# First batch of attention in native fp32, token-mixing weights converted at set steps, first q tile loaded from another queue

## Chip, core and metric

The kernel runs on one NeuronCore of a Trainium2 chip. The metric is the device time of one launch in microseconds (us), the median of several runs; lower is better. Engine names are those of the profile: PE is the matrix engine (PEld its weight load), DVE the vector engine, ACT the scalar engine, POOL the GpSimd engine, SP the engine whose queue issues most transfers.

## What is computed

Three stages run one after another on four sequences of 448 positions with 768 features: causal attention with 12 heads of 64, then a mixer (over positions, then over channels), then a second mixer with a cosine and a sine.

```python
scores = scale * np.matmul(q, k.transpose(0, 1, 3, 2))        # q, k, v: (4, 12, 448, 64)
scores = np.where(mask, -1000000000.0, scores)
attn = np.exp(scores - np.max(scores, axis=-1, keepdims=True))
attn = attn / (np.sum(attn, axis=-1, keepdims=True) + 1e-09)
x = np.matmul(attn, v)                                        # to (4, 448, 768)
...
h = np.maximum(xt @ w_tok1, 0.0) @ w_tok2                     # mixer 1, over positions
u = x + h.transpose(0, 2, 1)
x = u + np.maximum(u @ w_ch1, 0.0) @ w_ch2                    # mixer 1, over channels
...
theta = x @ w_theta                                           # mixer 2
y = einsum(w_tok_r, x * cos(theta)) + einsum(w_tok_i, x * sin(theta))
u = x + y
out = u + np.maximum(u @ w_ch, 0.0)
```

The weights arrive as 64-bit floats and are turned into 32-bit ones on the chip.

## The kernel before

**Attention.** Two heads make a pair, six pairs a batch, 24 pairs in all; they are numbered 0 to 23 (`b * NPR + pr`). A pair has seven score tiles (`TILES`), so batch 0 has 42 steps `n`. `prep` loads q, k and v of a pair one pair ahead. `scores` makes one tile: the matmul of q and k into a `sc` bank (three of them), on DVE the mask and the row maximum (L268), on ACT the exponential (L270). `pv` multiplies the exponentials with v, four steps later (`LAG`), `finish` normalizes a pair and splits it into a high and a low part, and `tokmix` does the token mixing after every second pair.

There are two ways of doing each of the two products. For a pair in `NATIVE`, q and k are used as fp32 tiles whose lower 64 partitions are set to zero by POOL (`k_pad`, `q_raw`), and one fp32 matmul per tile does the scores. For any other pair q and k are loaded twice over (128 partitions) and split on ACT and DVE into a high and a low part (`qs`, `kh`, `kl`), and two fp32r matmuls do them (L261 and L263). For a pair in `NATPV`, the exponentials are transposed on PE against an identity (L277), copied out of PSUM by ACT (L279, tile `ptf`), and multiplied by v in fp32 (L305). For any other pair ACT writes them as fp16 (`ph`), DVE writes the rest (L290), a transposing transfer on SP's queue turns them (L293, `pt<-ph`), v is split in three bfloat16 parts on DVE (`v_mid`), and PE does 83 small matmuls (L316).

Before the change pair 3 is not in `NATIVE` and pair 2 is not in `NATPV`; all others of the first batch are in both. `q_raw` and `k_raw` share two buffers (tag `qk_raw`), `k_pad` and `kh` another two.

**Weights.** `load64` loads a raw tile of 64-bit floats (two `raw` buffers) and converts it: one ACT operation (L124), four on DVE (L125, L126, L128, L129). `split_w` then makes the high part on ACT (L106) and the low part on DVE (L113). `tok_weights` does so for the four tiles of the token-mixing weights, `convert_early` for the first six tiles of the channel-mixing weights from step 21 on; later ones are converted as the channel mixing needs them. A channel weight is also stored (`w_c<-ws`) and streamed again for later batches.

**Order.** The Tile framework decides the order on each engine from a timeline that it works out itself when the program is built; `high_priority(AHEAD)` puts attention ahead, and `issue_after(x)` lets what is inside come only after x in that order. On the chip each engine then takes its instructions strictly in that order, and SP issues its transfers in its order too. The channel mixing of batch 0 (`run_units`) starts in the middle of batch 1; from there on PE has other work at hand whenever attention waits.

Of the kernel before, what the change touches and what calls it, by code (L numbers as in the profile page):

```python
# [13 lines left out]
AF = mybir.ActivationFunctionType  # L14
# [4 lines left out]
P = 128  # L19
B, H, S, D = 4, 12, 448, 64  # L20
E = H * D
NPR = H // 2
# [4 lines left out]
NEG = -1.0e30  # L27
PSC = 32768.0
BUFS = dict(ut=9, h2=6, acc=12, ws=4, wf=2, raw=2, sb=3, ph=3, pt=5)
NATIVE = {0, 1, 2, 4, 5, 6, 7}  # L30
NATPV = {0, 1, 3, 4, 5, 6, 7, 8, 9, 10, 11}
AHEAD, LAG, LOOK = 500, 4, 2
KEEP, UBACK = 6, 16
LATE_CONVERT = 16
EARLY = 6
ENGINES = {
    0: dict(qhi="A", qlo="D", khi="A", klo="D", v="D", phi="A", xhi="A", xlo="D", uhi="A", ulo="D"),
}
# [10 lines left out]
def fused(ctx, tc, q, k, v, w_tok1, w_tok2, w_ch1, w_ch2, w_theta, w_tok, w_ch, out):  # L49
# [15 lines left out]
    nc = tc.nc  # L65
# [114 lines left out]
    for j in range(BUFS["sb"]):  # L180
        sb = ac.tile([P, 512], F32, tag=f"sb{j}", name=f"sb{j}")
# [4 lines left out]
    def tok_weights(n):  # L186
        if n < 2:
            cols = slice(n * 512, (n + 1) * 512)
            load_split(wt1[:, :, cols], w_tok1[:, cols])
        else:  # L190
            load_split(wt2[:, n - 2], w_tok2[:, (n - 2) * S:(n - 1) * S])
# [7 lines left out]
    loads = {}  # L199

    def prep(b, pr):
        qr = ap2.tile([P, 2 * S], F32, tag="qk_raw", name="q_raw", bufs=2)
        if b * NPR + pr in NATIVE:
            kr = ap2.tile([P, 2 * S], F32, tag="kh", name="k_pad")
            for t, src in ((kr, k), (qr, q)):
                (nc.vector if b * NPR + pr == 0 and t is kr else nc.gpsimd).memset(t[64:128], 0.0)
                loads[b * NPR + pr] = nc.sync.dma_start(out=t[0:64], in_=src[b, pr, 0:64])
        else:
            loads[b * NPR + pr] = nc.sync.dma_start(out=qr, in_=q[b, pr])
            kr = ap2.tile([P, 2 * S], F32, tag="qk_raw", name="k_raw", bufs=2)  # L210
            nc.sync.dma_start(out=kr, in_=k[b, pr])
        vr = ap2.tile([P, 9 * D], F32, tag="v_raw", name="v_raw")
        nc.sync.dma_start(out=vr, in_=v[b, pr])
        if b * NPR + pr in NATIVE:
            qs, kh, kl = qr, kr, None
        else:
            qs = ap2.tile([P, 2 * S], F32R, tag="qs", name="qs")
            copy_to(pick("qhi"), qs, qr)
            rest_to(pick("qlo"), qs[64:128], qr[64:128], qs[64:128])
            kh = ap2.tile([P, 2 * S], F32R, tag="kh", name="kh")  # L220
            copy_to(pick("khi"), kh, kr)
            kl = ap2.tile([P, 2 * S], F32R, tag="kl", name="kl")
            rest_to(pick("klo"), kl, kr, kh)
        if b * NPR + pr in NATPV:
            return qs, kh, kl, (vr,)
        v1 = vr.bitcast(BF16).rearrange("p (n w) -> p n w", w=2)[:, :, 1]
        vm = ap2.tile([P, 9 * D], F32, tag="v_mid", name="v_mid", bufs=1)
        rest_to(pick("v"), vm, vr, v1)
        v2, v3 = (vm.bitcast(BF16).rearrange("p (n w) -> p n w", w=2)[:, :, z] for z in (1, 0))
        rest_to(pick("v"), v3, vm, v2)  # L230
        return qs, kh, kl, (v1, v2, v3)
# [3 lines left out]
    class Pair:  # L235
        def __init__(self, b, pr, parts):
# [4 lines left out]
            self.pts, self.ps = {}, None  # L241
            self.native_pv = b * NPR + pr in NATPV

    def scores(pp, i, h):
        ps = bank("sc", 3)
        if i == 0:
            j, kk, nb = 6, P, 2
            n = P if pp.kl is None else 256
            lhs = pp.qs[:, 0:P]
            cut = lambda t: t.rearrange("p (h s) -> p h s", h=2)[:, :, 0:n // 2]  # L250
            src = ps[:, 0:n].rearrange("p (h s) -> p h s", h=2)[:, :, 0:64]
            msk = mask0
        else:
            j, kk, nb = (i - 1) * 2 + h, 64 + P * i, 1 + 2 * i
            n = kk if pp.kl is None else max(256, kk)
            q0 = P * (3 * h + i)
            lhs = pp.qs[:, q0:q0 + P]
            cut = lambda t: t[:, h * S:h * S + n]
            src = ps[:, 0:kk]
            msk = mask[:, S - kk:S]  # L260
        nc.tensor.matmul(ps[:, 0:n], lhsT=lhs, rhs=cut(pp.kh), start=True, stop=pp.kl is None)  # L261
        if pp.kl is not None:
            nc.tensor.matmul(ps[:, 0:n], lhsT=lhs, rhs=cut(pp.kl), start=False, stop=True)  # L263
        sb = sbufs[count[0] % BUFS["sb"]]
        count[0] += 1
        full, sb = sb, sb[:, 64:512]
        dst = sb[:, 0:P].rearrange("p (h s) -> p h s", h=2) if i == 0 else sb[:, 0:kk]
        nc.vector.tensor_tensor_reduce(out=dst, in0=src, in1=msk, op0=ALU.add, op1=ALU.min, scale=-0.125,  # L268
                                       scalar=3.0e38, accum_out=pp.mx[:, j:j + 1])
        nc.scalar.activation(sb[:, 0:kk], sb[:, 0:kk], AF.Exp, bias=pp.mx[:, j:j + 1], scale=-1.0,  # L270
                             accum_out=pp.sm[:, j:j + 1])
        if pp.native_pv:
            nt = 1 + i
            c0 = 64 if i == 0 else 0
            pst = mm_bank()
            for u in range(nt):
                nc.tensor.transpose(pst[:, u * P:(u + 1) * P], full[:, c0 + u * P:c0 + (u + 1) * P], ident)  # L277
            pt = ap2.tile([P, 4, P], F32, tag="pt", name="ptf", bufs=BUFS["pt"])
            nc.scalar.activation(pt[:, 0:nt].rearrange("p n q -> p (n q)"), pst[:, 0:nt * P], AF.Copy)  # L279
            pp.pts[i, h] = pt  # L280
            return
        ph = ap2.tile([P, 2 * S], F16, tag="ph", name="ph", bufs=BUFS["ph"])
        if i == 0:
            hi, los = ph[:, 0:P], ((ph[:, P:2 * P], 0, P),)
        else:
            hi = ph[:, 64:64 + kk]
            los = ((ph[:, 0:64], 0, 64), (ph[:, 64 + kk:2 * kk], 64, kk))
        copy_to(pick("phi"), hi, sb[:, 0:kk], PSC)
        for dst, c0, c1 in los:
            nc.vector.scalar_tensor_tensor(out=dst, in0=sb[:, c0:c1], scalar=PSC, in1=hi[:, c0:c1],  # L290
                                           op0=ALU.mult, op1=ALU.subtract)
        pt = ap2.tile([P, 7, P], F16, tag="pt", name="pt", bufs=BUFS["pt"])
        nc.sync.dma_start_transpose(out=pt[:, 0:nb, :], in_=ph[:, 0:nb * P])  # L293
        pp.pts[i, h] = pt
# [109 lines left out]
    def convert_early(n):  # L404
        while early[0] < min(n, EARLY):
            convert(*jobs[early[0]])
            early[0] += 1
# [24 lines left out]

    eng, turn = dict(ENGINES[0]), {}

# [6 lines left out]
    pairs, xgs = {}, {}  # L441
# [12 lines left out]
    for n, (b, pr, t) in enumerate(steps):  # L454
# [3 lines left out]
            pairs[b, pr] = Pair(b, pr, parts[b, pr])  # L458
        with tc.high_priority(AHEAD):
            scores(pairs[b, pr], *TILES[t])  # L460
        if b == 0 and n % 3 == 2 and n // 3 < 4:
            tok_weights(n // 3)
        if n >= 21:
            convert_early((n - 18) // 3)
        if n >= 140:
# [126 lines left out]
    for b in range(B):  # L592
        raw, x2 = [], []
        for d in range(DT):
            r = acc_tile()
            nc.sync.dma_start(out=r, in_=x2d[b][d])
            t = hl_tile("ut")
# [126 lines left out]
```

## Time and profile before

| | us |
|---|---|
| median of 3 runs | 936.4 (933.72 to 938.17) |
| the profiled execution, its own time | 932.47 |
| its span, first to last instruction | 930.7 |
| granted clock of PE over the span | 0.996 |

The profiled execution lies 3.9 us below the median of the runs and 1.25 us below the lowest of them. Outside its span lie 1.8 us. All rows below are of this one execution, in us from the start of its span. An fp32 matmul with fp32 operands leaves two records on PE, so "x8" of such a line is four matmuls; an fp32r matmul or a transpose leaves one.

### The profile page before, as it was taken

How to read it: one execution, taken by the hardware profiler on the slowest of the kernel's cores; microseconds unless marked ns; L12 is line 12 of the kernel's file. 1: busy time of each engine (PE TensorE's matmuls, PEld its weight loads, DVE VectorE, ACT ScalarE, POOL GpSimd, SP SyncE). 2: the span in 40 equal slices, each digit the busy share in tenths (PEclk: the TensorE clock that was granted, in tenths of full speed). 3: DMA queues.
4: the chain of work that ended last, by engine and by line, in shares of the span. 5: the costliest groups of instructions: out<-in, count | busy, mean ns of one | idle time of the engine just before them, and what ended most of it. 6: DMA issues, size and time to landing. Idle time of an engine off the chain costs nothing.

```text
span 930.7 us, 16002 instructions
## 1 busy us (share of the span) xinstructions
PE 901.3 (97%) x5846; PEld 822.5 (88%) x5846; DVE 637.1 (68%) x1484; ACT 389.5 (42%) x916; POOL 107.3 (12%) x176
## 2 busy tenths in 40 slices
PE   7799999999999989899999999999999999999998
PEld 5687899999988879798989899999999999999997
DVE  5998579999777776757776278855765467475351
ACT  5886676667555555435544043322211212112100
POOL 2110000000000000000000000021531243242120
PEclk9999999999999999999999999999999999999999
DMA  5888567887999988999699989863604235153043
GB/s 170 244 248 314 220 237 237 319 284 246 264 257 335 250 220 191 236 291 251 197 309 275 318 290 355 303 206 109 208 1 151 61 112 168 28 162 111 22 131 128
DMA packets 108335, 196.75 MB, mean 211 GB/s; under 512 B 65120, under 2 KB 77152, under 8 KB 108256
## 3 DMA queue, kind: packets, MB, share of 16 engines
q1 hardware_dynamic: 107104, 194.15, 68.3%
q0 software_dynamic: 1152, 1.57, 0.8%
q8 instruction: 46, 0.75, 0.3%
q14 instruction: 33, 0.27, 0.1%
HBM read 145.88 MB, written 34.60 MB: 194 GB/s over the span
## 4 chain that ended last, share of the span: by engine, by line
PE 74%; DMA 15%; DVE 7%; issue 2%; ACT 1%; SPq 1%; DVEq 0%; ACTq 0%
PE ps_mm L162 17%; PE ps_mm L160 17%; PE ps_mm L161 17%; DMA pt<-ph 11%; PE ps_pv L305 4%; PE ps_sc L261 3%; PE ps_sc L162 3%; PE ps_sc L160 3%; PE ps_sc L161 3%; PE ps_mm L277 2%; PE ps_pv L316 2%; DMA x2d<-acc 1%; DVE sb L268 1%; PE ps_sc L263 1%; DVE ph L290 1%
## 5 line engine op out<-in xcount | busy, mean ns | idle before, releaser
L162 PE MATMUL ps_mm<-h,ws 128*128 128x448 f32 x432 | 159.1, 369 | 0.0
L161 PE MATMUL ps_mm<-h,ws 128*128 128x448 f32 x432 | 158.9, 368 | 0.0
L160 PE MATMUL ps_mm<-h,ws 128*128 128x448 f32 x432 | 158.7, 368 | 0.0
L161 PE MATMUL ps_mm<-ut,ws 128*128 128x448 f32 x288 | 107.0, 372 | 0.0
L162 PE MATMUL ps_mm<-ut,ws 128*128 128x448 f32 x288 | 106.9, 372 | 0.0
L160 PE MATMUL ps_mm<-ut,ws 128*128 128x448 f32 x288 | 106.5, 371 | 0.0
L270 ACT ACTIVATE sb<-sb,mx 128x192 f32<-128x192 f32 (+3 forms) x168 | 89.1, 532 | 33.4 <-DVE mx L268 32.9
L162 PEld LDWEIGHTS ps_mm<-h,ws 128*128 128x128 f32 x432 | 81.2, 188 | 7.0
L161 PEld LDWEIGHTS ps_mm<-h,ws 128*128 128x128 f32 x432 | 81.2, 188 | 6.9
L160 PEld LDWEIGHTS ps_mm<-h,ws 128*128 128x128 f32 x432 | 81.1, 188 | 6.9 <-DVE h L378 0.2
L268 DVE CUSTOM_DVE_ANT_0 sb<-ps_sc,mask 128x192 f32<-128x192 f32 (+3 forms) x168 | 74.3, 456 | 11.5 <-PE ps_mm L277 7.2
L290 DVE SCALAR_TENSOR_TENSOR ph<-sb,ph 128x64 f16<-128x64 f32 (+3 forms) x169 | 46.2, 316 | 42.3 <-ACT ph L106 42.1
L109 POOL TENSOR_SCALAR ut<-acc 128x448 fp32r<-128x448 f32 x24 | 16.7, 704 | 472.6 <-DMA acc<-x2d 462.6
L528 ACT ACTIVATE tmp<-ps_sc 128x384 f32<-128x384 f32 x28 | 13.5, 483 | 132.3 <-PE ps_sc L162 132.1
L106 ACT ACTIVATE ph<-sb 128x192 f16<-128x192 f32 (+3 forms) x91 | 39.5, 443 | 67.8 <-DMA pt<-ph 67.3
L305 PE MATMUL ps_pv<-v_raw,ptf 128*128 128x128 f32 (+1 forms) x418 | 57.6, 276 | 2.1 <-ACT ptf L279 1.8
L160 PEld LDWEIGHTS ps_mm<-ut,ws 128*128 128x128 f32 x288 | 54.4, 189 | 5.1 <-DMA ws<-w_c 0.4
L305 PEld LDWEIGHTS ps_pv<-v_raw,ptf 128*128 128x128 f32 x418 | 53.3, 191 | 6.2 <-ACT ptf L279 3.8
L161 PEld LDWEIGHTS ps_mm<-ut,ws 128*128 128x128 f32 x288 | 54.5, 189 | 4.7 <-issue 0.2
L162 PEld LDWEIGHTS ps_mm<-ut,ws 128*128 128x128 f32 x288 | 54.4, 189 | 4.8 <-issue 0.4
L316 PEld LDWEIGHTS <-pt 128*128 128x128 f16 x1079 | 35.8, 97 | 20.5 <-DMA pt<-ph 11.9
L386 DVE TENSOR_TENSOR acc<-ps_mm,acc 128x448 f32<-128x448 f32 x48 | 29.8, 622 | 30.9 <-PE ps_mm L162 30.6
(151 smaller groups left out, 2097.6 us busy)
## 6 DMA issues: line engine op xcount, KB each, us to landing
ws<-w_c SPq DMA_DIRECT2D x102, 768.0 KB, 5.6
raw<-in_w_ch_dram SPq DMA_DIRECT2D x30, 768.0 KB, 5.7
w_c<-ws SPq DMA_DIRECT2D x30, 768.0 KB, 5.1
q_raw<-in_q_dram SPq DMA_DIRECT2D x17, 448.0 KB, 5.0
k_raw<-in_k_dram SPq DMA_DIRECT2D x17, 448.0 KB, 4.6
v_raw<-in_v_dram SPq DMA_DIRECT2D x24, 288.0 KB, 4.6
x2d<-acc SPq DMA_DIRECT2D x24, 224.0 KB, 5.2
acc<-x2d SPq DMA_DIRECT2D x24, 224.0 KB, 4.0
```

The source lines that it names most:

```text
L106: nc.scalar.activation(dst, src, AF.Copy, scale=scale)
L160: nc.tensor.matmul(ps, lhsT=ka(a[:, 0]), rhs=kb(b[:, 0]), start=first, stop=False)
L161: nc.tensor.matmul(ps, lhsT=ka(a[:, 0]), rhs=kb(b[:, 1]), start=False, stop=False)
L162: nc.tensor.matmul(ps, lhsT=ka(a[:, 1]), rhs=kb(b[:, 0]), start=False, stop=last)
L261: nc.tensor.matmul(ps[:, 0:n], lhsT=lhs, rhs=cut(pp.kh), start=True, stop=pp.kl is None)
L268: nc.vector.tensor_tensor_reduce(out=dst, in0=src, in1=msk, op0=ALU.add, op1=ALU.min, scale=-0.125, scalar=3.0e38, accum_out=pp.mx[:, j:j ...
L270: nc.scalar.activation(sb[:, 0:kk], sb[:, 0:kk], AF.Exp, bias=pp.mx[:, j:j + 1], scale=-1.0, accum_out=pp.sm[:, j:j + 1])
L277: nc.tensor.transpose(pst[:, u * P:(u + 1) * P], full[:, c0 + u * P:c0 + (u + 1) * P], ident)
L290: nc.vector.scalar_tensor_tensor(out=dst, in0=sb[:, c0:c1], scalar=PSC, in1=hi[:, c0:c1], op0=ALU.mult, op1=ALU.subtract)
L305: nc.tensor.matmul(pp.ps[:, reg:reg + n], lhsT=pt[:, u], rhs=pp.v[0][:, vt * D:vt * D + n], start=(u == 0), stop=(u == len(blks) - 1))
L316: nc.tensor.matmul(pp.ps[:, reg:reg + D], lhsT=pt[:, blk], rhs=pp.v[c][:, vt * D:(vt + 1) * D], start=(n == 0), stop=(n == len(jobs) - 1))
L386: nc.vector.tensor_tensor(out=acc[d], in0=ps[:, 0:S], in1=acc[d], op=ALU.add)
```

## The change

Pair 3 enters `NATIVE` and pair 2 enters `NATPV`, so all six pairs of batch 0 do both products in fp32. `tok_weights` is called at steps 3, 5, 8 and 10 instead of 2, 5, 8 and 11, and each call may only come behind that step's exponential. The first q tile is loaded in two pieces from ACT's queue instead of in one from SP's.

```diff
-NATIVE = {0, 1, 2, 4, 5, 6, 7}
-NATPV = {0, 1, 3, 4, 5, 6, 7, 8, 9, 10, 11}
+NATIVE = {0, 1, 2, 3, 4, 5, 6, 7}
+NATPV = {0, 1, 2, 3, 4, 5, 6, 7, 8, 9, 10, 11}
...
+TOK_STEPS = (3, 5, 8, 10)
...
                 (nc.vector if b * NPR + pr == 0 and t is kr else nc.gpsimd).memset(t[64:128], 0.0)
-                loads[b * NPR + pr] = nc.sync.dma_start(out=t[0:64], in_=src[b, pr, 0:64])
+                if b * NPR + pr == 0 and t is qr:
+                    for c in (slice(0, 2 * P), slice(2 * P, 2 * S)):
+                        nc.scalar.dma_start(out=t[0:64, c], in_=src[b, pr, 0:64, c])
+                else:
+                    loads[b * NPR + pr] = nc.sync.dma_start(out=t[0:64], in_=src[b, pr, 0:64])
...
-        nc.scalar.activation(sb[:, 0:kk], sb[:, 0:kk], AF.Exp, bias=pp.mx[:, j:j + 1], scale=-1.0,
+        pp.last = nc.scalar.activation(sb[:, 0:kk], sb[:, 0:kk], AF.Exp, bias=pp.mx[:, j:j + 1], scale=-1.0,
...
-        if b == 0 and n % 3 == 2 and n // 3 < 4:
-            tok_weights(n // 3)
+        if n in TOK_STEPS:
+            with tc.issue_after(pairs[b, pr].last.ins):
+                tok_weights(TOK_STEPS.index(n))
```

The changed program's lines stand one to six numbers higher than those of before (L124 becomes L125, L279 becomes L284, L270 becomes L275). From about the first third of the channel mixing of batch 0 on, the two programs have the same order on every engine; all that moves lies ahead of it.

On DVE at the very start, from the third score tile of pair 0 on, first before and then changed (L268, changed L273, is the mask and maximum of a score tile; `wf` is the token weight under conversion):

```order
12 L125 TENSOR_SCALAR wf<-wf 128x512
13 L126 TENSOR_SCALAR wf<-wf 128x512
14 L268 ISA sb_148,mx<-ps_sc,mask 128x320
15 L268 ISA mx 128x1
16 L268 ISA sb_150,mx<-ps_sc,mask 128x320
17 L268 ISA mx 128x1
```

```order
12 L273 ISA sb_148,mx<-ps_sc,mask 128x320
13 L273 ISA mx 128x1
14 L273 ISA sb_150,mx<-ps_sc,mask 128x320
15 L273 ISA mx 128x1
16 L273 ISA sb_152,mx<-ps_sc,mask 128x448
17 L273 ISA mx 128x1
18 L126 TENSOR_SCALAR wf<-wf 128x512
```

Three score tiles have moved ahead of the first conversion of a weight.

On ACT in pair 2, around the first two channel weights, first before and then changed (L106 is the fp16 exponentials, the split q and the high part of a weight; L284 the copy of transposed exponentials out of PSUM):

```order
34 L270 ACTIVATE sb_152,sm<-sb_152,mx 128x128
35 L124 ACTIVATE wf<-raw 128x768
36 L106 ACTIVATE ph<-sb_152 128x128
37 L279 ACTIVATE ptf<-ps_mm 128x512
38 L106 ACTIVATE qs<-q_raw 128x896
39 L270 ACTIVATE sb_148,sm<-sb_148,mx 128x192
40 L279 ACTIVATE ptf<-ps_mm 128x512
41 L106 ACTIVATE ph<-sb_148 128x192
```

```order
36 L275 ACTIVATE sb_152,sm<-sb_152,mx 128x128
37 L125 ACTIVATE wf<-raw 128x768
38 L284 ACTIVATE ptf<-ps_mm 128x512
39 L275 ACTIVATE sb_148,sm<-sb_148,mx 128x192
40 L284 ACTIVATE ptf<-ps_mm 128x512
41 L284 ACTIVATE ptf<-ps_mm 128x128
42 L107 ACTIVATE wt_147<-wf 128x448
43 L275 ACTIVATE sb_150,sm<-sb_150,mx 128x192
44 L275 ACTIVATE sb_152,sm<-sb_152,mx 128x320
45 L284 ACTIVATE ptf<-ps_mm 128x256
46 L125 ACTIVATE wf<-raw 128x768
```

The fp16 copies and the split of q are gone, the copies `ptf` of pair 2 have come in, and the first channel weight keeps its place right behind the first exponential of pair 2.

On SP at the same place, first before and then changed (L211 loads k of pair 3, L293 is a transposing transfer, L121, changed L122, loads a raw weight):

```order
11 L121 DMA raw<-in_w_ch_dram 128x1536
12 L209 DMA q_raw<-in_q_dram 128x896
13 L121 DMA raw<-in_w_ch_dram 128x1536
14 L293 DMA_TRANSPOSE pt<-ph 128x2x128
15 L213 DMA v_raw<-in_v_dram 128x576
16 L211 DMA k_raw<-in_k_dram 128x896
17 L293 DMA_TRANSPOSE pt<-ph 128x3x128
```

```order
8 L218 DMA v_raw<-in_v_dram 128x576
9 L212 DMA k_pad<-in_k_dram 64x896
10 L212 DMA q_raw<-in_q_dram 64x896
11 L122 DMA raw<-in_w_ch_dram 128x1536 x2
12 L218 DMA v_raw<-in_v_dram 128x576
13 L212 DMA k_pad<-in_k_dram 64x896
14 L212 DMA q_raw<-in_q_dram 64x896
15 L122 DMA raw<-in_w_ch_dram 128x1536
```

The changed rows begin with v of pair 2: k and q of pair 3 (9 and 10) now stand ahead of the first two raw channel weights, k and q of pair 4 (13 and 14) ahead of the third, and the seven transposing transfers are gone.

## Rows read from the trace of the kernel before

**Rows 1.** The page, busy time of PE over the span: us, share, instructions.

```profile
PE 901.3 (97%) x5846; PEld 822.5 (88%) x5846; DVE 637.1 (68%) x1484; ACT 389.5 (42%) x916; POOL 107.3 (12%) x176
```

**Rows 2.** Windows of 10 us: length, busy us by engine, granted clock, DMA.

```profile
core 0: us, PE busy (x) PEld busy (x) DVE busy (x) ACT busy (x) POOL busy (x), PEclk, DMA share, GB/s
0.00:10.00 10.00, 4.52 (x12) 3.29 (x13) 2.37 (x11) 2.65 (x7) 4.48 (x16) 1.00 0.80 222
10.00:20.00 10.00, 8.94 (x63) 7.58 (x62) 8.06 (x26) 8.07 (x23) 1.91 (x2) 1.00 0.45 129
20.00:30.00 10.00, 9.29 (x63) 7.34 (x61) 9.92 (x29) 8.84 (x25) 0.00 (x0) 1.00 0.59 200
30.00:40.00 10.00, 6.36 (x43) 4.23 (x43) 9.86 (x29) 7.41 (x19) 1.63 (x2) 1.00 0.82 213
40.00:50.00 10.00, 9.23 (x78) 8.61 (x78) 9.68 (x27) 7.54 (x19) 0.84 (x1) 0.83 1.12 264
...
70.00:80.00 10.00, 9.02 (x63) 7.99 (x62) 7.81 (x19) 6.95 (x15) 0.00 (x0) 1.00 0.72 257
100.00:110.00 10.00, 10.00 (x60) 9.16 (x60) 4.59 (x13) 6.09 (x14) 0.00 (x0) 1.00 0.22 73
```

**Rows 3.** The window with a lower granted clock, same columns.

```profile
40.27:43.68 3.41, 3.09 (x20) 3.10 (x21) 3.41 (x9) 2.42 (x6) 0.84 (x1) 0.50 1.08 288
```

**Rows 4.** Timeline of the start (start, length, engine, work), and k's landing time.

```profile
0.76 0.58 SPq L207 DMA_DIRECT2D k_pad<-in_k_dram  x1
1.39 0.57 SPq L207 DMA_DIRECT2D q_raw<-in_q_dram  x1
5.48 5.04 PE L261 MATMUL ps_sc<-k_pad,q_raw 128*128 128x128 f32 x12 [5.48 <-DMA q_raw<-in_q_dram]
k_pad<-in_k_dram SPq DMA_DIRECT2D x1, 224.0 KB, 3.5
```

**Rows 5.** Waits from 0 to 75 us: who for whom, us in total, times, longest.

```profile
DVE wf L125 <- ACT wf L124: 6.1, 3, 3.3
...
ACT wf L124 <- DMA raw<-in_w_ch_dram: 4.1, 3, 2.7
...
PE ps_pv L316 <- DMA pt<-ph: 2.5, 4, 0.9
...
PE ps_mm L160 <- ACT h L344: 1.0, 1, 1.0
```

**Rows 6.** The chain that ended last, of PE's own pieces: start, us, what.

```profile
18.31 0.44 PE ps_mm L277 x4
...
19.29 0.89 PE ps_pv L305 x8
...
20.51 0.75 PE ps_sc L261 x2
...
103.84 0.21 PE ps_mm L162
```

**Rows 7.** Window of pair 2's fp16 product, line L316 alone: PE, then weight loads.

```profile
30.00:54.00 24.00, 4.53 (x83) 3.32 (x83) 0.93 0.95 237
```

**Rows 8.** DVE work of the two pairs: L290 in its window, split k, split v.

```profile
30.00:54.00 24.00, 3.49 (x13) 0.93 0.95 237
L113 DVE TENSOR_TENSOR kl<-k_raw,kh 128x896 fp32r<-128x896 f32 x1 | 1.1, 1081 | 0.0
L113 DVE TENSOR_TENSOR v_mid<-v_raw x1: 756/756/756, 26.7 to 26.7; 128x576 f32<-128x576 f32 x1
```

**Rows 9.** Transfers issued from 0 to 80 us: count, KB, median us to landing.

```profile
raw<-in_w_ch_dram SPq DMA_DIRECT2D x8, 768.0 KB, 4.8
...
q_raw<-in_q_dram SPq DMA_DIRECT2D x1, 448.0 KB, 6.9
```

**Rows 10.** Timeline, k of pair 3: its issue on SP, and ACT's wait for it.

```profile
34.22 0.38 SPq L211 DMA_DIRECT2D k_raw<-in_k_dram  x1
38.44 0.95 ACT L106 ACTIVATE kh<-k_raw 128x896 fp32r<-128x896 f32 x1 [1.08 <-DMA k_raw<-in_k_dram]
```

## Prediction

> **What bounds the kernel now.** I read the page first, then windows of 10 us, then the waits and the chain in the windows that stand out. On the page PE is busy for 97% of the span [rows 1], so a change pays only where PE stands still or runs slowly. The windows say where that is: from 100 us on PE is busy for all of a window, but in the first 80 us it is not. It lacks 5.48 us in the first window, 1.06 in the second, 0.71, 3.64, 0.77 and, from 70 to 80 us, 0.98 [rows 2]. DVE is the fullest engine there, with 9.92, 9.86 and 9.68 of 10 us from 20 to 50 us [rows 2]. One stretch of 3.41 us at 40 us has a granted clock of 0.50, the 1.2 GHz level [rows 3]; it follows the window in which PE was idle most, and costs half its length, 1.7 us. So there is a ledger for this stage: what PE gets back of these gaps, less the work that PE is given in addition. Behind 100 us both programs do the same work in the same order on a full PE, and I carry the difference through to the end unchanged.
>
> **What the edits cost PE.** Pair 2 gets 19 transposes and 19 fp32 products. Four transposes take 0.44 us and four products 0.89 us in the chain [rows 6], so that is 2.1 + 4.2 us. It loses 83 small matmuls; their weight loads were busy for 3.32 us [rows 7], partly at the low clock, and I take 2.5 us for them. That is +3.8 us. Pair 3's scores have 128 + 2 x (192 + 320 + 448) = 2048 columns in fp32; 448 of them take 0.75 us [rows 6], so all take 3.4 us. Before they were two passes over 2304 columns, at 0.21 us for 448 [rows 6]: 2.2 us. That is +1.3 us. Together PE gets **+5.1 us**, between 4.3 (if the small matmuls cost the whole 3.3) and 5.4.
>
> **What the edits take away elsewhere.** DVE loses 13 operations of L290 (3.49 us), two splits of v of about 0.76 us, and the splits of q and k of about 1.08 us each [rows 8]: 7.2 us of the engine that is full. ACT swaps seven fp16 copies and two splits for seven copies out of PSUM; I put nothing for that, since ACT is busy for at most 8.84 of 10 us there [rows 2]; the cover is gone where ACT's queue itself stands still, which is the third rival. POOL clears two more tiles, while it is busy for 0.0 to 1.6 us in those windows [rows 2]. ACT issues two transfers at the start, 0.58 us each if it takes as long as SP [rows 4]; nothing waits for ACT before PE's first scores are done, after 5 us, which hides them. SP loses seven transposing transfers and gains nothing but k and q of pair 3 as fp32 tiles instead of raw ones.
>
> **What PE gets back.** (1) The start. PE's first matmul at 5.48 us waits for q; k was issued at 0.76 us and landed after 3.5 us, at 4.3 us [rows 4]. With q's first piece issued at the same time from ACT, k lands last: 5.48 less some 4.4 is 1.1 us. If only the earlier place counts, it is the 0.63 us between the issues of k and q. I take 0.8 us. (The Trainium skill, "DMA: Bandwidth & Descriptors", section "Issuing engines are not separate DMA queues", says that transfers of all issuing engines interleave on the same 16 DMA engines, so that a second issuer saves only the time of issuing. By that rule the term would be the 0.63 us alone and the sum 0.2 us smaller; the 0.58 us that SP took for one issue agree.) (2) The wait behind the first token weight. DVE waits up to 3.3 us for ACT's L124 [rows 5] with ready score tiles behind it; in the changed order three score tiles come first. PE lacks 1.06 us in that window [rows 2]; I take 1.0. (3) Pairs 2 and 3. PE waits 2.5 us for transposed exponentials [rows 5], and pair 3 cannot start its scores before k has come, which was issued only at 34.22 us, when pair 2's scores had freed the buffer, and reached ACT at 38.44 us [rows 10]. Both go: k and q of pair 3 have a buffer as soon as pair 1 is done. Of the 3.64 us in the window from 30 to 40 us I take 3.4, of the 0.77 behind it 0.7, of the 0.71 ahead of it 0.5. (4) With that idle time the low clock goes: 1.7 us. (5) A little, 0.3 us, for the smaller tile of work on DVE from 50 us on. Sum: 0.8 + 1.0 + 3.4 + 0.7 + 0.5 + 1.7 + 0.3 = **8.4 us**. At the least it is 3.4 (only the 2.5 of waits for transposes, and half of the first two terms); at the most all 12.6 us that the windows show to 80 us, without the 4.4 us in which nothing has landed, and 1.7 us for the clock, 9.9 us.
>
> **What comes in its place.** The raw channel weights. There are two raw buffers, a raw tile takes 4.8 us to land [rows 9], and ACT meets its L124 in strict order. Before, ACT waited 4.1 us for such tiles in this stage, and through one of these waits (2.7 us) PE lost 1.0 us at the token mixing [rows 5]. After the change ACT comes to the first channel weight sooner, for the fp16 copies and the split of q ahead of and around it are gone, but the load doesn't leave sooner: it still waits for the raw buffer, and on SP it stands behind k and q of pair 3 (later ones behind those of pairs 4, 5 and 6), which wait for the last scores of the pair before. So ACT will stand there longer, with the copies `ptf` and the exponentials queued behind, for which PE's products and transposes wait, and DVE's token mixing behind those. I reckon with ACT waits of 7 to 8 us in place of 4.1; at PE's 1.0 us for each 4.1 that is **+0.8 us**, between nothing and 4 us (each of four such waits costing PE 1.0).
>
> **The sum.** -8.4 + 5.1 + 0.8 = -2.5 us. The profiled execution would go from 932.47 to 930.0 us. It lies 3.9 us under the median of the runs; the same step from the median gives 936.4 - 2.5 = **933.9 us**.
>
> **Rivals.**
> A. *DVE sets the pace, and all its relief is gained.* DVE is busy for 98% of the time from 20 to 50 us, and 7.2 us less work there, with the 1.8 us of the start, would end the stage up to 9 us earlier. PE's ledger stands against it: with all 9.9 us back and 4.3 to 5.4 us more work it gains 4.5 to 5.6 us, unless the records of busy PE hide idle time, as they can, since matmuls overlap. Time: 5 to 9 us less, 927 to 931.5, with 929.5 as its middle. (This is the rule of the Trainium skill, "Perfetto Trace Analysis", section "Identifying the Most-Contended Engine", to relieve the engine with the highest occupancy first; by it DVE's 7.2 us would count in full. That DVE is the fullest engine there the trace bears out; that nothing else would hold the stage it does not.)
> B. *The gain is eaten.* The stage goes on at the pace of the raw weights: each load waits for its buffer and for the next pair's k and q. The early start is lost at the first channel weight, since that load leaves no sooner, and the new waits cost PE 3 to 4 us instead of 0.8. Then -8.4 + 5.1 + 3.5 is no change: 936.6, from 935 to 939.
> C. *Slower.* The same place, ACT's L125 (before L124) behind a late raw tile, becomes the bound. Four loads follow one another through the two buffers; if each takes 6.9 us, as a q of 448 KB did at this place, instead of 4.8 [rows 9], the chain grows by 4 x 2.1 = 8.4 us, against the 2.5 us gained: 5.9 us slower, 942. It decides from about 6.6 us a load on ((2.5 + 4.7) / 4 above 4.8). Seven transfers fewer in the queues speak against it.
>
> **How the numbers follow.** About 0.5% (4.7 us) is what a measurement of this kernel can tell from no change. Chances: the forecast with up to 4.7 us gained 0.45, A 0.35, B 0.12, C 0.08. The forecast alone spans 932 to 936. The range must take in A down to a gain of 9 us and some of B, up to 3 us slower than the median: 926.5 to 939.5, which leaves out C and the edges. Faster by over 0.5% is A, 0.35; slower is C, 0.08; the rest, 0.57, is within 0.5%.
>
> **What would show it.** Right: PE's first matmul at 4.4 to 4.9 us; no wait of DVE of 3 us at the first L126; PE busy for over 9 of 10 us in the window from 30 to 40 us and no granted clock of 0.50 there; k of pair 3 issued at some 22 us; ACT waiting for raw channel weights 7 us or more in the first 80 us; the first channel mixing matmul some 2.5 us earlier than before, and the rest of the trace shifted by that. Wrong: if ACT's waits for raw weights stay at 4 us or less, A is right; if PE shows idle time of more than 4 us behind them, B or C. Also wrong if the stalls in the later batches move by more than the shift, since I carry that part over unchanged.

## The result, and the profile after

The changed kernel is slower: 941.03 us, median of 22 runs (935.76 to 943.92), against 936.37 us of 22 runs of the kernel before on the same chips. The ratio is 1.0059, its 95% interval 1.0043 to 1.0074, which is 5.5 us (the two medians alone differ by 4.7; the text goes by the ratios). The forecast was 933.9 us with a range to 939.5; it was wrong in sign. The profiled execution has a span of 939.2 us, 8.5 more than before; 3.9 of that are due to before's profiled execution, which lay so far under its median.

The page of the changed kernel, against [rows 1]:

```profile
PE 908.0 (97%) x5820; PEld 828.7 (88%) x5820; DVE 631.4 (67%) x1467; ACT 388.9 (41%) x914; POOL 109.3 (12%) x178
```

The windows of the changed kernel, to be read against [rows 2]:

```profile
core 0: us, PE busy (x) PEld busy (x) DVE busy (x) ACT busy (x) POOL busy (x), PEclk, DMA share, GB/s
0.00:10.00 10.00, 5.08 (x12) 3.58 (x13) 2.37 (x11) 2.65 (x7) 4.49 (x16) 1.00 0.80 210
10.00:20.00 10.00, 9.79 (x66) 8.10 (x64) 8.20 (x24) 7.21 (x21) 1.90 (x2) 1.00 0.43 133
20.00:30.00 10.00, 9.10 (x63) 7.17 (x60) 8.68 (x30) 7.78 (x23) 1.63 (x2) 1.00 0.71 188
30.00:40.00 10.00, 7.05 (x35) 5.30 (x35) 5.76 (x15) 6.21 (x17) 0.74 (x1) 0.83 0.32 113
40.00:50.00 10.00, 7.11 (x54) 6.82 (x54) 6.62 (x16) 4.80 (x11) 0.89 (x2) 0.93 0.70 220
50.00:60.00 10.00, 9.96 (x61) 8.64 (x61) 9.38 (x23) 7.50 (x18) 0.00 (x0) 0.89 0.85 308
60.00:70.00 10.00, 9.39 (x59) 7.16 (x57) 9.26 (x27) 6.72 (x19) 1.81 (x2) 1.00 0.71 224
70.00:80.00 10.00, 7.43 (x57) 6.81 (x58) 8.96 (x20) 8.62 (x21) 1.63 (x2) 1.00 0.90 286
```

The first two windows improved as forecast (PE 5.08 after 4.52, 9.79 after 8.94). But from 30 to 50 us every engine is idle for a part of the time: PE lacks 5.8 us there (4.4 before), and DVE, full before, 7.6. The clock is low twice. The two stretches, against the one of [rows 3]:

```profile
34.97:38.38 3.41, 3.41 (x13) 2.70 (x12) 2.03 (x5) 2.94 (x9) 0.00 (x0) 0.51 0.00 0
48.70:52.11 3.41, 3.41 (x12) 3.15 (x13) 3.17 (x7) 1.41 (x3) 0.00 (x0) 0.50 0.36 110
```

The waits from 0 to 75 us, against [rows 5]:

```profile
ACT wf L125 <- DMA raw<-in_w_ch_dram: 10.8, 3, 4.0
DVE wf L126 <- ACT wf L125: 9.5, 5, 3.3
...
PE ps_pv L310 <- ACT ptf L284: 5.8, 5, 3.0
...
PE ps_mm L161 <- ACT h L349: 2.9, 1, 2.9
```

ACT waits 10.8 us for raw channel weights, not 4.1. Where that strikes PE is seen in the timelines of ACT and PE (in square brackets the idle time ahead and its releaser):

```profile
32.29 0.89 ACT L125 ACTIVATE wf<-raw 128x768 f32<-128x768 f32 x1 [3.69 <-DMA raw<-in_w_ch_dram]
...
33.72 1.16 PE L310 MATMUL ps_pv<-v_raw,ptf 128*128 128x128 f32 x8 [2.95 <-ACT ptf L284]
...
47.39 0.89 ACT L125 ACTIVATE wf<-raw 128x768 f32<-128x768 f32 x1 [4.03 <-DMA raw<-in_w_ch_dram]
...
48.61 0.69 PE L161 MATMUL ps_mm<-wt,h 128*128 128x448 f32 x1 [2.89 <-ACT h L349]
```

ACT stands at a raw tile for 3.69 and 4.03 us; the copy (or the ReLU `h`) that PE needs is the next thing in ACT's queue, so PE idles 2.95 and 2.89 us; and soon behind each of these gaps, 1.25 and 0.09 us after its end, begin 3.41 us of PE's work at the low clock. A third such wait, at 70 us, costs PE 1.55 us.

Why the tiles are late, in the timelines of SP and DVE:

```profile
24.44 0.59 SPq L212 DMA_DIRECT2D q_raw<-in_q_dram  x1
...
25.11 0.63 DVE L130 SCALAR_TENSOR_TENSOR wf<-raw,wf 128x448 uint32<-128x448 uint32 x1
...
25.80 5.05 SPq L122 DMA_DIRECT2D raw<-in_w_ch_dram  x2
...
39.33 0.96 DVE L130 SCALAR_TENSOR_TENSOR wf<-raw,wf 128x768 uint32<-128x768 uint32 x1
...
39.75 0.59 SPq L212 DMA_DIRECT2D q_raw<-in_q_dram  x1
...
40.51 0.46 SPq L122 DMA_DIRECT2D raw<-in_w_ch_dram  x1
```

L130 is DVE's last operation on a raw tile. The first raw channel weight leaves at 25.80 us, 0.06 us after the L130 that ends at 25.74 and frees its buffer; the third leaves 0.2 us after the L130 that ends at 40.29, eight us after ACT had begun on the tile that this L130 finishes. The q of pair 4 ahead of the third load on SP was being issued until 40.34, so for the third load this trace alone does not tell the buffer from SP's order. Before, the first left at 23.33 and the third at 39.82 us; ACT, which had more to do, came to the third only at 45.57 and found it there.

Over all eight the transfers are a little slower than before (median 5.4 us; 4.8 in [rows 9]; 0 to 80 us), but the two that ACT waits for are among the slow ones. The eight, then the first and the third alone:

```profile
raw<-in_w_ch_dram SPq DMA_DIRECT2D x8, 768.0 KB, 5.4
...
raw<-in_w_ch_dram SPq DMA_DIRECT2D x1, 768.0 KB, 6.4
...
raw<-in_w_ch_dram SPq DMA_DIRECT2D x1, 768.0 KB, 6.8
```

Before, these two took 5.1 and 5.7 us. So the first tile landed 3.8 us later than before, 2.5 by its buffer and 1.3 by its transfer; the third 1.8 us later, 0.7 and 1.1. Why these two transfers took longer is not shown. PE starts earlier (against [rows 4]):

```profile
0.75 1.20 ACTq L210 DMA_DIRECT2D q_raw<-in_q_dram  x2
...
4.92 1.09 PE L266 MATMUL ps_sc<-k_pad,q_raw 128*128 128x128 f32 x3 [4.92 <-DMA k_pad<-in_k_dram]
```

The first matmul of channel mixing, PE's first on `ut`, is a good mark for the end of the stage: 103.27 us before, 110.44 after, 7.2 us later. Of the 8.5 us by which the spans differ only 1.3 come behind it.

### The profile page after: what moved, and what is told of

The parts are those of the page before. It is cut to its first block, busy times and chain, and to the rows that moved or that the text cites. A ratio compares the mean times of both kernels' runs of the same rounds, so it can differ in the third digit from the quotient of the medians.

```text
span 939.2 us, 15916 instructions
## 1 busy us (share of the span) xinstructions
PE 908.0 (97%) x5820; PEld 828.7 (88%) x5820; DVE 631.4 (67%) x1467; ACT 388.9 (41%) x914; POOL 109.3 (12%) x178
## 4 chain that ended last, share of the span: by engine, by line
PE 75%; DMA 11%; issue 6%; DVE 5%; ACT 2%; POOL 0%; SPq 0%; DVEq 0%; ACTq 0%
PE ps_mm L161 17%; PE ps_mm L163 17%; PE ps_mm L162 17%; DMA pt<-ph 7%; PE ps_pv L310 4%; PE ps_sc L266 3%; PE ps_sc L163 3%; PE ps_sc L161 3%; PE ps_sc L162 3%; PE ps_mm L282 2%; DMA raw<-in_w_ch_dram 2%; PE ps_pv L321 1%; DVE ph L295 1%; PE ps_sc L268 1%; PE ps_mm L346 1%
## 5 line engine op out<-in xcount | busy, mean ns | idle before, releaser
L275 ACT ACTIVATE sb<-sb,mx 128x192 f32<-128x192 f32 (+3 forms) x168 | 89.4, 535 | 33.9 <-DVE mx L273 33.4
L273 DVE CUSTOM_DVE_ANT_0 sb<-ps_sc,mask 128x192 f32<-128x192 f32 (+3 forms) x168 | 74.0, 456 | 15.7 <-PE ps_mm L282 12.1
L295 DVE SCALAR_TENSOR_TENSOR ph<-sb,ph 128x64 f16<-128x64 f32 (+3 forms) x156 | 42.8, 317 | 46.1 <-ACT ph L107 46.0
L310 PE MATMUL ps_pv<-v_raw,ptf 128*128 128x128 f32 (+1 forms) x456 | 63.5, 279 | 7.1 <-ACT ptf L284 5.8
L310 PEld LDWEIGHTS ps_pv<-v_raw,ptf 128*128 128x128 f32 x456 | 58.9, 194 | 12.0 <-ACT ptf L284 8.6
L107 ACT ACTIVATE ph<-sb 128x192 f16<-128x192 f32 (+3 forms) x84 | 36.6, 444 | 67.5 <-DMA pt<-ph 66.9
L541 ACT ACTIVATE tmp<-tmp 128x384 f32<-128x384 f32 x28 | 14.8, 527 | 86.3 <-DVE tmp L539 86.3
```

The costliest lines, as they stand in the source:

```text
L107: nc.scalar.activation(dst, src, AF.Copy, scale=scale)
L275: pp.last = nc.scalar.activation(sb[:, 0:kk], sb[:, 0:kk], AF.Exp, bias=pp.mx[:, j:j + 1], scale=-1.0, accum_out=pp.sm[:, j:j + 1])
L310: nc.tensor.matmul(pp.ps[:, reg:reg + n], lhsT=pt[:, u], rhs=pp.v[0][:, vt * D:vt * D + n], start=(u == 0), stop=(u == len(blks) - 1))
```

## Experiments

Each kernel was timed against the kernel before on the same chip; the median of before lay between 934.5 and 936.4 us there, so the ratios are what to compare. "Mark" is the first matmul of channel mixing in the profiled execution, "third" the time at which ACT begins on the third raw channel weight. Both are of one execution, which can lie some us from the median of its kernel: u_q's took 946.4 us, 6.4 more than its median; x_both's and u_q1's took 2.5 and 2.2 us less than theirs.

| kernel | us (runs) | ratio, 95% interval | third | mark |
|---|---|---|---|---|
| before | 936.4 (22) | 1 | 45.57 | 103.27 |
| changed | 941.0 (22) | 1.0059, 1.0043 to 1.0074 | 47.39 | 110.44 |
| u_tok | 937.5 (12) | 1.0026, 1.0007 to 1.0045 | 38.68 | 104.55 |
| u_pv | 945.7 (6) | 1.0105, 1.0074 to 1.0136 | 50.12 | 112.52 |
| u_nat | 945.9 (6) | 1.0106, 1.0075 to 1.0137 | 44.07 | 112.37 |
| u_q | 940.0 (12) | 1.0046, 1.0023 to 1.0068 | 48.40 | 113.53 |
| u_q1 | 942.7 (6) | 1.0077, 1.0050 to 1.0104 | 45.70 | 108.81 |
| c_rawtok | 937.3 (12) | 1.0014, 1.0000 to 1.0028 | 39.97 | 103.99 |
| c_kqpool | 938.9 (12) | 1.0027, 1.0010 to 1.0044 | 45.42 | 108.10 |
| x_both | 938.7 (12) | 1.0039, 1.0016 to 1.0062 | 42.38 | 106.57 |
| x_pace | 938.7 (12) | 1.0025, 1.0006 to 1.0045 | 40.54 | 106.06 |
| c_raw4 | 935.7 (12) | 1.0007, 0.9987 to 1.0026 | 39.21 | 103.39 |
| n_raw4 | 935.6 (12) | 1.0010, 0.9993 to 1.0026 | 36.36 | 101.15 |
| f_nat | 937.3 (12) | 1.0019, 1.0003 to 1.0035 | 40.62 | 105.55 |
| f_tok | 940.3 (12) | 1.0053, 1.0031 to 1.0075 | 55.78 | 111.61 |
| f_tokq | 938.5 (12) | 1.0038, 1.0022 to 1.0054 | 52.14 | 107.79 |
| f_q | 941.2 (12) | 1.0064, 1.0040 to 1.0087 | 47.13 | 112.13 |
| f_q2sp | 940.3 (12) | 1.0044, 1.0022 to 1.0067 | 48.99 | 108.14 |
| f_q1act | 941.8 (9) | 1.0078, 1.0050 to 1.0106 | 48.77 | 111.98 |
| b_rawtok | 941.3 (8) | 1.0065, 1.0042 to 1.0088 | 48.17 | 110.17 |

**Theory and rivals.** My theory after the result: the two raw buffers come free late, the raw channel weights land late, and ACT, in its strict order, holds up PE. Rival W: PE's 5.1 us of additional work are the loss. Rival S: the loads are late because k and q stand ahead of them on SP. Rival P: the new place of the token weights delays everything.

**u_tok**, the token weights' steps undone:

```diff
-        if n in TOK_STEPS:
-            with tc.issue_after(pairs[b, pr].last.ins):
-                tok_weights(TOK_STEPS.index(n))
+        if b == 0 and n % 3 == 2 and n // 3 < 4:
+            tok_weights(n // 3)
```

> The changed kernel with one part undone: the token weights are called at steps 2, 5, 8 and 11 again and do not wait for an exponential. My theory (two raw buffers are held until the last conversion on DVE, so the raw channel weights come late, and ACT stands at L125 with the copies for PE behind it): the buffers still turn over as before, so the time stays within 1.5 us of the changed kernel's 941.0. Rival P (the new place of the token weights delays the buffers and with them everything): the wait of 3.7 us at the first channel weight goes and the time falls by 3 us or more, to 938 or less. Rival W (only PE's 5.2 us of additional work counts): 941, no change.

3.1 us came back (ratio 1.0026), the mark moved from 110.44 to 104.55. P was right, and my theory wrong in saying that the buffers would turn over as before: ACT begins on the first token weight at 10.47 us (12.48 in the changed kernel), the first raw channel weight leaves at 22.86 (25.80), the third at 33.80 (40.51). A delay of 2 us at the first weight has grown to 6.7 by the third load.

**c_rawtok**, a buffer of their own for the last two token weights:

```diff
-            load_split(wt2[:, n - 2], w_tok2[:, (n - 2) * S:(n - 1) * S])
+            f = wf_tile()[:, 0:S]
+            load64(f, w_tok2[:, (n - 2) * S:(n - 1) * S], ap2.tile([P, S, 2], U32, tag="kl", name="raw2"))
+            split_w(wt2[:, n - 2], f)
```

> The changed kernel with the raw tiles of the last two token weights in a buffer of their own (that of kl, which nothing uses before pair 8), so that the two raw buffers are free for the first channel weights some 8 us earlier; no work is added or taken away. My theory: the first channel weight is issued at 17 to 20 us instead of 25.8, ACT's wait of 3.7 us there and PE's 2.95 us behind it go, the later ones shrink, and the time falls by 3 to 6 us, to 935 to 938. Rival W (PE's work): 941. Rival S (the raw loads are late because they stand behind k and q of the next pair on SP): the third load, which still stands behind k and q of pair 4, stays as late as it was, and at most half of it comes back, 938 to 940.

As my theory had it: ratio 1.0014, 4.2 us less than the changed kernel. The first channel weights leave at 16.70 us. The third load, which rival S wanted as late as it was, leaves at 34.27 us and not at 40.51, although q of pair 4 still stands right ahead of it on SP:

```profile
16.70 2.94 SPq L122 DMA_DIRECT2D raw<-in_w_ch_dram  x2
...
33.10 0.55 SPq L214 DMA_DIRECT2D q_raw<-in_q_dram  x1
34.27 0.33 SPq L122 DMA_DIRECT2D raw<-in_w_ch_dram  x1
```

The windows from 20 to 60 us are full, with no low clock:

```profile
20.00:30.00 10.00, 9.62 (x70) 8.36 (x69) 9.92 (x33) 9.69 (x29) 1.63 (x2) 1.00 0.53 163
30.00:40.00 10.00, 9.93 (x73) 8.60 (x72) 9.72 (x22) 6.81 (x19) 1.62 (x2) 1.00 0.60 179
40.00:50.00 10.00, 9.75 (x64) 8.06 (x63) 9.04 (x23) 8.71 (x22) 0.01 (x1) 1.00 0.82 294
50.00:60.00 10.00, 9.60 (x71) 8.24 (x70) 9.97 (x27) 7.73 (x21) 1.77 (x2) 1.00 0.80 271
```

**c_kqpool**, k and q of pairs 2 to 5 issued by POOL:

```diff
-                    loads[b * NPR + pr] = nc.sync.dma_start(out=t[0:64], in_=src[b, pr, 0:64])
+                    loads[b * NPR + pr] = (nc.gpsimd if b == 0 and pr > 1 else nc.sync).dma_start(out=t[0:64], in_=src[b, pr, 0:64])
```

> The changed kernel with k and q of the fp32 pairs 2 to 5 issued from POOL's queue, right behind POOL's own clearing of the tiles, so that no raw load stands behind them on SP. Rival S (order on SP): the third raw load leaves 1 to 3 us earlier, the waits shrink, 2 to 5 us less, 936 to 939. My theory: the loads leave when DVE's last conversion (L130) frees the buffer, at 25.8 and 40.5 us as before, and the time stays within 1.5 us of 941.0.

The time, 938.9, lies where S put it, and my theory's time is missed. But the first raw load left no earlier (26.26 us). The third left 1.7 us earlier, at 38.82, and again right behind the L130 that frees its buffer, which ends at 38.76 here and at 40.29 in the changed kernel:

```profile
37.81 0.95 DVE L130 SCALAR_TENSOR_TENSOR wf<-raw,wf 128x768 uint32<-128x768 uint32 x1
...
38.82 0.33 SPq L122 DMA_DIRECT2D raw<-in_w_ch_dram  x1
```

The order on DVE had changed too: a normalization (L328) that comes before this L130 in the changed kernel comes behind it here. So 1.5 of the 1.7 us come with the buffer, and SP's order can have held the third load by no more than the remaining 0.2 us. S is out as the holder of both loads; by which of its differences this kernel is 3.0 us faster than the changed one is not shown.

**u_pv** and **u_nat**, one set undone each: `NATPV` without 2, `NATIVE` without 3.

> The changed kernel with pair 2 taken out of NATPV again: its second product goes over fp16 and transposing transfers, PE has 3.8 us less work, SP seven transposes more. Rival W (only PE's work counts): 3.8 us less, 937.2. My theory: the raw loads still pace the stage, and the transposes share the queues with them, so less than half of it comes back, 939 to 941.

> The changed kernel with pair 3 taken out of NATIVE again: its scores go over split fp32r tiles, PE has 1.3 us less work, DVE and ACT some 4 us more between them, and k of pair 3 waits for its buffer again. Rival W (only PE's work counts): 941.0 less 1.3 is 939.7. My theory (the raw loads wait for DVE's last conversion in the buffer, and ACT stands at them in its order): DVE has more to do ahead of that conversion, so nothing is gained: 941 to 944.

Both are about 4.4 us slower than the changed kernel, with 3.8 and 1.3 us less work on PE. That is the end of rival W, and more than my theory expected. Either one set is worth more than it costs once the other parts are there, or the order that comes out with one set alone is a worse one; these two runs do not tell which.

**u_q**, the first q tile back on SP in one piece, and **u_q1**, on ACT's queue in one piece.

```diff
-                    for c in (slice(0, 2 * P), slice(2 * P, 2 * S)):
+                    for c in (slice(0, 2 * S),):
```

> The changed kernel with the first q tile on SP's queue again, in one piece. The earlier start was 0.56 us at PE's first matmul (5.48 to 4.92). If the start is kept to the end: 0.5 us slower, 941.5. If it is lost at the first raw channel weight, as my theory has it (that load leaves when DVE frees the buffer): no difference, 941.0. Both are close to what can be told; the first matmul of channel mixing in the trace tells more: 111.0 by the one, 110.4 by the other, after 110.44 in the changed kernel.

> The changed kernel with the first q tile in one piece on ACT's queue. SP's order is the same to the last transfer, the orders on PE, DVE and ACT differ. If the 5.5 us of the change are of the parts themselves: 940 to 942 again. If they depend on the order that comes out, the time may land anywhere from 936 to 942, and where it is lower, ACT's waits at raw tiles from 28 to 50 us (7.7 us in the changed kernel) are shorter too.

u_q is not told from the changed kernel; its mark, 113.53, is later than either view had it, but it is of the long execution named above and settles nothing. In u_q1 SP's order is the same and the loss stays, with the same two waits of ACT (3.46 us at 31.77, 2.78 at 45.70): the loss of the changed kernel does not hang on one order on PE.

**x_both** (c_rawtok and u_tok together) and **x_pace** (c_rawtok, `(n - 18) // 4` for `(n - 18) // 3`).

> The changed kernel with the raw tiles of the last two token weights in a buffer of their own, as in c_rawtok, and the token weights at the steps of before, without a wait for exponentials, as in u_tok. If the two take away the same wait (buffers held too long), the gains do not add: 937 to 938, as either alone. If they take away different waits, they add to 7 us: 934, which would be below the kernel before.

> c_rawtok with the six early channel weights spread over more steps, one in four instead of one in three, from step 22 to step 42. What is left of the waits there is ACT's 2.6, 1.3 and 0.6 us for the raw tiles at 61 to 75 us, and PE lacks 3.7 us from 60 to 100 us. My theory: a slower pace lets the loads land before ACT comes to them, and 1 to 3 us of this come back, 934.5 to 936.5. Rival W: PE is full in any case, no difference, 937.3.

The two gains do not add; x_both, 1.0039, is if anything slower than either edit alone. That fits their taking away the same wait, but does not show it: with both, ACT still waits 2.2 and 2.3 us for the third and fourth tile, and the order is another again. x_pace missed: ACT's longest wait for a raw tile grew to 3.7 us (2.6 in c_rawtok), and its time is not told from c_rawtok's. A later conversion frees its buffer later, which would explain the wait.

**c_raw4** and **n_raw4**. c_raw4 is c_rawtok, and the third and fourth channel weight land in halves in the idle `kl` and `qs` tiles (a conversion in halves, used where `early[0] in (2, 3)`); n_raw4 has the same buffers in f_nat.

```diff
+        raws = [ap2.tile([P, m, 2], U32, tag=t, name=f"raw_{t}") for t in ("kl", "qs")]
+        for z, raw in enumerate(raws):
+            nc.sync.dma_start(out=raw.rearrange("p n w -> p (n w)"), in_=src[:, z * m:(z + 1) * m].bitcast(U32))
```

> c_rawtok, and in addition the third and fourth channel weight land in halves in the idle buffers of kl and qs, so that in effect four raw buffers serve the early weights; the work grows by three operations of ACT and DVE for each of the two. My theory (raw tiles that come late are what the changed kernel lost): ACT's waits at raw tiles to 60 us are under 1 us in sum, PE lacks less than 1 us in 30 to 60 us, channel mixing starts at 101 to 103 us (before 103.27, c_rawtok 103.99), and the time is 934 to 937. If it is no faster than c_rawtok (937.3 or more), the late raw tiles are all gone there already and the rest is PE's additional work.

> f_nat (both sets changed, token weights and q as before) with the four raw buffers of c_raw4. My theory: its waits for raw tiles (7.3 us of ACT, 3.2 us of PE behind them) go, channel mixing starts at 102 to 104 us instead of 105.55, and the time is 933 to 936. If 937 or more, the raw tiles were not what f_nat lost by.

With four buffers the loss is gone: 1.0007 and 1.0010, no difference from before. (c_raw4 is not told from c_rawtok, and its mark came 0.4 us later than expected.) In n_raw4 the mark is 101.15, 2.1 us *earlier* than before although PE has 5.1 us more work: 7.2 us of PE's time were got back. Its stage:

```profile
20.00:30.00 10.00, 10.00 (x74) 8.79 (x73) 9.96 (x31) 9.39 (x28) 1.63 (x2) 1.00 0.66 199
30.00:40.00 10.00, 9.49 (x66) 7.72 (x64) 9.92 (x22) 8.08 (x22) 2.04 (x2) 1.00 0.81 258
40.00:50.00 10.00, 10.00 (x70) 8.85 (x69) 10.00 (x27) 8.44 (x21) 0.00 (x0) 1.00 0.59 224
```

These 2.1 us don't reach the end. From the mark to the last matmul its profiled execution takes 5.2 us more than that of before, of which 2.0 are the amount by which before's lay under its median in that call; the growth lies between 246 and 461 us, in attention of later batches. The fp16 products that begin at 246.2 us before begin 2.1 us earlier here, those of 457.3 us begin 3.1 us later. Why is open.

**The parts by themselves**, on the kernel before: f_nat (both sets), f_tok (token steps), f_q (first q tile), f_tokq (both of these); each is its part of the change's diff.

> The kernel before with the two sets alone changed: pair 3 in NATIVE and pair 2 in NATPV; token weights and first q tile as before. If these two parts are what makes the change slow (5.2 us more work on PE and no gain): 940 to 941.5. My theory, from undoing either (4.7 us slower each) and from undoing the token steps (3.1 us faster): these parts by themselves cost 1 to 2 us at most, 936 to 938.

> The kernel before with the token weights' steps and their wait for an exponential alone; no transfer and no amount of work changes, only the order. If a different order is enough to lose what the kernel before has (as f_q2sp suggests): 938 to 942 where before is 935. If the steps are harmless and what f_tokq lost came from the first q tile: 934 to 936.

> The changed kernel with both sets undone, so the kernel before with the token weights' steps and the first q tile's queue alone changed. My theory: the token weights behind their exponentials let the raw buffers go later, the first raw channel weight leaves some 2 us later than before, and that costs 2 to 5 us: 938 to 941. If the steps do no harm by themselves: 935.5 to 936.5.

> The kernel before with the first q tile alone in two pieces on ACT's queue. PE's first matmul comes 0.5 to 0.9 us earlier, at 4.6 to 5.0 us. If the earlier start is kept: 935.3. If it is lost at the first raw channel weight: 936, no difference; channel mixing starts at 103.3 in the trace then, against 102.6.

The sets alone cost 1.8 us, the token steps alone 5.0, the q tile alone 6.0. They don't add: f_tok and f_q together, f_tokq, cost 3.6. That f_q is as slow as the whole change I had not expected; three more runs on the kernel before look into it: **f_q2sp** (the first q tile in two pieces, on SP's queue), **f_q1act** (in one piece, on ACT's), **b_rawtok** (c_rawtok's buffer alone).

```diff
-                loads[b * NPR + pr] = nc.sync.dma_start(out=t[0:64], in_=src[b, pr, 0:64])
+                for c in ((slice(0, 2 * P), slice(2 * P, 2 * S)) if b * NPR + pr == 0 and t is qr else (slice(0, 2 * S),)):
+                    loads[b * NPR + pr] = nc.sync.dma_start(out=t[0:64, c], in_=src[b, pr, 0:64, c])
```

> The kernel before with the first q tile in two pieces, but both on SP's queue as before. No transfer changes its queue and no work is added beyond one issue; but the order that the framework works out changes in pairs 2 to 5. If the order alone makes f_q slow (6 us): channel mixing starts 3 us or more later than before here too, and the time is 937 to 941 where before is 935. If ACT's queue makes f_q slow: 935, no difference.

> The kernel before with the first q tile in one piece on ACT's queue. The order differs from that of before in a tenth as many places as that of f_q. If ACT's queue makes f_q slow: 938 or more. If the order does: it lies nearer to before, 934 to 937, with PE's first matmul 0.4 to 0.7 us earlier.

> The kernel before with the one part of c_rawtok: the last two token weights land in the idle kl tiles. ACT waited 6.7 us for raw tiles there in 0 to 75 us. If late raw tiles bound the kernel before as well: 2 to 4 us faster, 931 to 933. If DVE, full from 20 to 50 us, bounds it in that stretch: no difference, 934 to 936.

All three are 4 to 7 us slower, and f_tok, which changes no transfer and no work, 5.0. ACT's queue is not needed for the loss (f_q2sp), and fewer differences in the order are no protection (f_q1act, a miss). What they share is another order of pairs 2 and 3. And b_rawtok is the very edit that brought the changed kernel 4.2 us (c_rawtok); on the kernel before it costs 6.1. In before, PE's longest wait for a transposed `pt` is 0.9 us [rows 5]; it is 3.0 us in f_q, 4.1 in f_q1act, 3.9 in b_rawtok, and in f_tok, by its waits from 0 to 80 us:

```profile
PE ps_pv L317 <- DMA pt<-ph: 6.3, 2, 5.3
...
PE ps_pv L306 <- ACT ptf L280: 4.2, 3, 3.3
```

In f_q2sp it is 1.1 us, and its loss is spread over smaller gaps; a single cause for all of them is not shown.

This limits what the runs on the changed kernel say. Every edit moves the order, and the order alone moves the time by as much as most of these runs gained. That the late raw tiles cost the changed kernel its time rests on the waits in its trace, and on kernels in which more buffers took away the waits for channel weights up to 60 us: c_rawtok and c_raw4, whose times fell as expected, and n_raw4, whose mark came 4.4 us earlier than f_nat's (their times are not told apart). How much of each gain is the buffer and how much another order is not separated.

## Why the prediction was wrong

**PE's additional work** was not what decided: undoing either set, and the 3.8 or 1.3 us with it, made the kernel slower still. Its size was right: on the page PE's busy time rose by 6.7 us (901.3 to 908.0), of which some 1.7 are the longer low clock, which leaves 5.0.

**What PE gets back** was right as an amount that is there, and wrong for this kernel. The start, term (1), brought 0.56 us for 0.8, and the window of term (2) 0.85 for 1.0. Without the late raw tiles n_raw4 got 7.2 us back; the terms (3) to (5), which apply to it, promised 6.6. That the two lie so close is in part luck, as n_raw4 has two more buffers for the early weights, with which the terms did not reckon. In the changed kernel PE's busy time in the first 80 us fell from 66.70 to 64.91 us, the low clock doubled from 3.41 to 6.8 us (1.7 us more lost), and PE had 5.1 more to do. With the 1.8 that is 8.6; the mark moved by 7.2, and the 1.4 between them are not accounted for.

**The step that failed is "What comes in its place"**, +0.8 us. It named the place (ACT at L125, the copies behind it) but mis-sized it: behind the three waits for raw tiles PE lost 2.95, 2.89 and 1.55 us, 7.4 in place of the 1.0 of before, so 6.4 us where the forecast added 0.8. Three things in it were wrong. It said that the first raw load "doesn't leave sooner"; it left 2.5 us later: with the three score tiles and their exponentials ahead of the first token weight, ACT begins on that weight at 12.48 us (10.49 before), and every conversion behind it, and with it both buffers, comes later. With the steps alone undone (u_tok) the load leaves at 22.86. I had booked that same move as a gain of 1.0 us, term (2). It put the cause on SP's order besides the buffer; the measured holder is the buffer, until DVE's L130 (c_kqpool). And it priced ACT's wait at a quarter of its length for PE, from one case before; here 3.69 and 4.03 us cost PE 2.95 and 2.89, and a low clock behind each. So term (4), that the low clock goes, reversed.

**Rival C** gave 942, and 0.08: right in time and place, wrong in mechanism. It wanted four loads of 6.9 us, 8.4 us more than before; they took 6.4, 4.9, 6.8 and 4.2 us, 2.5 more than before (5.1, 4.4, 5.7, 4.6). So slower transfers are a part of it, but not the 8.4. At the first tile ACT came at 28.60 us (before 27.80) and the tile 3.8 us later than before. At the third ACT, relieved of work, came 2.2 us earlier (43.36 for 45.57) and the tile 1.8 us later.

**Rival A** rested on DVE as the fullest engine. DVE's busy time over the span fell by 5.7 us (637.1 to 631.4; 7.2 had been worked out), in the first 80 us by 7.5 (66.72 to 59.23), as some of its work came later; and the stage got longer. The Trainium skill, "Perfetto Trace Analysis", section "Identifying the Most-Contended Engine", would relieve the fullest engine first; here the trace does not bear it out by itself: what DVE gained it spent waiting, 9.5 us at L126 for ACT (6.1 before).

**The tacit step**: I took the order of before as neutral and the parts as terms of a sum. Five small changes ahead of pair 2 (f_tok, f_q, f_q2sp, f_q1act, b_rawtok) cost 4.1 to 7.3 us each; the order of before is a favourable one among the neighbours that were run. An edit there can put that at stake, whatever it does itself, and the forecast had no term for it.

## What to carry to other kernels

Where a short ring of buffers is filled by one queue and drained in strict order by several engines, ask of every moved piece of work when it lets the buffer go, not only when it starts: 2 us of delay at the first conversion became 6.7 us at the third channel load, and moving two tiles into idle buffers went with 4.2 us less in the changed kernel, though with 6.1 more in the kernel before. Where a framework works out the order, measure a few small changes first; their spread (here 4 to 7 us, all to the worse) is the yardstick for a forecast of 2.5. And no version that was run beats the kernel before; c_raw4 and n_raw4 equal it.

## What was unexpected of the hardware

The earlier start comes from the two pieces, not from the second queue. PE's first matmul stood at 5.48 us with q in one piece on SP; at 4.62 with two pieces on SP (f_q2sp), 4.63 and 4.92 with two on ACT (f_q, changed); and at 5.64 and 6.06 with one piece on ACT (u_q1, f_q1act). With q undivided on ACT's queue, k, issued at the same time, took 5.2 and 4.7 us to land (f_q1act, u_q1), where it took 3.5 before. The Trainium skill, "DMA: Bandwidth & Descriptors", section "Issuing engines are not separate DMA queues", says that transfers started by different engines run on the same 16 DMA engines and interleave. These landing times agree.

In the changed kernel the two gaps of 2.9 us on PE were each followed by 3.41 us at a granted clock of 0.50; in c_rawtok, whose longest gap from 10 to 80 us was 1.6 us, the clock stayed at 1.00 there. But no long gap is needed: in the kernel before no gap between 10 us and the low stretch at 40.27 us was longer than 1.0 us, while PE was busy for only 6.36 of the 10 us from 30 to 40 [rows 2].
